# A sequence-mixing layer and a gated feed-forward on one core: another order for the opening

## The chip, the cores and the metric

The kernel runs on one core of a Trainium2 chip. The metric is the device time of one execution in microseconds; of several runs the median is given. A core has five engines with an instruction queue each, which work side by side and wait for each other through semaphores: TensorE (PE: matrix multiplications into PSUM), VectorE (DVE) and ScalarE (ACT) for elementwise work, GpSimd (POOL), and SyncE (SP), which here only issues DMA transfers. The output's transfers are issued from ScalarE's queue (L625).

## The reference, cut to what matters

A linear recurrence with a complex decay per channel, then a feed-forward whose hidden value is the product of two projections:

```python
mag = np.sqrt(a_re * a_re + a_im * a_im)
scale = np.minimum(mag, 0.999) / (mag + 1e-06)
a_re_n, a_im_n = (a_re * scale, a_im * scale)
...
for t in range(S):
    ar, ai = (a_re_n[:, :, t, :, None], a_im_n[:, :, t, :, None])
    new_re = ar * S_re - ai * S_im
    new_im = ar * S_im + ai * S_re
    kv = np.einsum('bhd,bhe->bhde', k[:, :, t], v[:, :, t])
    S_re, S_im = (new_re + kv, new_im)
    y[:, :, t] = np.einsum('bhd,bhde->bhe', q[:, :, t], S_re)
...
a = x @ w_a
b = x @ w_b
return (a * b @ w_out).astype(np.float32)
```

There are 4 sequences of 768 steps with 8 heads of 48 channels (3072 tokens of 384 values), a hidden width of 1536, and everything is float32.

## The kernel before, in words

The work is cut into 12 units (NU): two sequences by a chunk of 128 steps each. A unit goes through three parts.

*The elementwise part*, `prep(u)`, is VectorE's, with some ScalarE. `scale(u)` (L166) makes the factor that limits |a| from logarithms and exponentials: seven ScalarE instructions and five VectorE ones (L178, L185, L188, L190, L192), on a scratch tile `tmp`; for unit 0 in two halves. Then z = a * scale (L210), the running products of z over 16 steps (L223 to L234, one multiplication L226 and one addition L232 for each step; for unit 0 each in two halves), products over the blocks of 16 (L253, L259), their combination (L274, L279), an inverse square (L282 to L305), and q and k multiplied by the running products and their inverse (L294, L309). From unit 2 on, a unit's scale is made inside the part of the unit before it: in `prep(u)`, `scale(u + 1)` is drawn on by the loop over the 16 steps (L214, L234), with unit u's `a_t` as scratch. For units 0 and 1 this isn't so: unit 0's scale is issued by itself, and unit 1's stands at the head of `prep(1)` (L202, L203), with unit 0's `a_t` (`a_first`) as scratch. A unit's last act is to load `a_t` two units ahead (L317).

*The stacking and the attention*. `stack(u)` (L323) moves the products from 128 partitions, where heads cross partition borders, to one head per slice of `stk`, by ten DMA transfers from SBUF to SBUF, all issued by SyncE. `attn(u)` (L350) then yields after each of 18 pieces: scores (L364, masked on VectorE at L367), transposes (L375), outputs (L404), the rounding rest of the outputs (L412, L415), and the state for the next chunk (L423, L430).

*The feed-forward*, `gemm1` and `gemm2` for each of 12 blocks f of the hidden width (NF): 18 matmuls (L467) make a and b, ScalarE and VectorE make the product h and split it into a rounded value and a rest (L475 to L478), and six more matmuls (L485) add it to the output. Each operand is given to TensorE as two float32r parts, a rounded value and a rest, so the weights have to be split as well.

That splitting, `split_weights`, is a generator with one yield for each block f. A block has three parts (of w_a, w_b and w_out). For each, VectorE rebuilds the words with three instructions (L133, L135, L137; here called a conversion), ScalarE rounds (L141), TensorE subtracts (L146, L147), and ScalarE rounds the rest (L148). The words come by `load_weights(f)` (L121), three DMA transfers of 384 KB for a block.

The instructions are issued in the text's order to a tile framework, which allocates buffers, sets the semaphores and lays out each engine's queue; `tc.high_priority` moves a block of instructions ahead in that. The text's order around the change is this. Loads (L584 to L592): a of unit 0, weights of block 0, q and k of unit 0, block 1, v of unit 0, block 2, a of unit 1, then blocks 3 to 11. Then `scale(0)`, `prep(0)`, `stack(0)`, the load of q and k of unit 1, and the conversions of six blocks (CONV_FIRST). Then the pieces of `attn(0)`, with a part of `prep(1)` after each: `drain(gen, ns)` (L594) draws on a generator until the costs that it yields, in nominal ns, add up to ns; that is P1_A = 800 here. In the first turn of the main loop (w = 0) each block f is preceded by the next block's conversion and P1_F = 3000 of `prep(1)`; at f = P1_AT = 4 the rest of `prep(1)`, `stack(1)`, the load of q and k of unit 2 are issued and `prep(2)` is set up. `slot()` issues pieces of `attn(1)` from then on, spread over the blocks up to f = 11, where `prep(2)` and `stack(2)` are issued as a whole (L661 to L668). In later turns `prep` is drawn on by 2400 a block.

Of the kernel before, what the change touches and what calls it, by code (L numbers as in the profile page):

```python
# [22 lines left out]
NU = NBP * NCH  # L23
# [11 lines left out]
EPS = 1e-6  # L35
A2_MAX = 2.0 ** 60
ST = 8
P1_A = 800
P1_F = 3000
TOK = 2 * C  # L40
RUN = 2 * TOK + 2
NF = DF // 128
# [5 lines left out]
NCHK = NU * G + NU + 1  # L48
WPART = ((0, DM), (DM, DM), (2 * DM, DM))
CONV_FIRST = 6  # L50
P1_AT = 4
MOE_FIRST = 4000
ATTN_FIRST = 2000
ATTN_AT = (5, 6, 6, 6, 6)
# [12 lines left out]
def tile_kernel(ctx: ExitStack, tc: tile.TileContext, a_d, qk_d, v_d, w_d, qn_d, kn_d, vn_d, an_d, out_d):  # L67
    nc = tc.nc
    vec, act, pe, sync = nc.vector, nc.scalar, nc.tensor, nc.sync
# [35 lines left out]
    stk = const.tile([128, H, RUN], F32, name="stk")  # L105
    nc.gpsimd.memset(stk[KS:128], 0.0)
    qk = const.tile([128, NJ, 2, RUN], F32, name="qk")
# [13 lines left out]
    def load_weights(f):  # L121
        for m, (c0, n) in enumerate(WPART):
            raws[f, m] = wpool.tile([128, n, 2], U32, name=f"w{m}{f}")
            sync.dma_start(out=raws[f, m].rearrange("p c s -> p (c s)"),
                           in_=w_d[f, :, c0:c0 + n].bitcast(U32))
# [28 lines left out]
    def load_a(u):  # L154
        t = apool.tile([128, 2, W], F32, name="a_t")
        for hs in halves if u == 0 else (slice(0, W),):
            sync.dma_start(out=t[:, :, hs], in_=a_d[u, :, :, hs])
        return t

    a_tiles = {}  # L160
# [5 lines left out]
    def scale(u, a_t, tmp):  # L166

        sc = zpool.tile([128, W], F32, name="sc")
        for n, hs in enumerate(halves if u == 0 else (slice(0, W),)):
            n = n and NU
            t = tmp[:, 0:2, hs]
            m, x, s0 = t[:, 0], t[:, 1], sc[:, hs]
            act.activation(out=t, in_=a_t[:, :, hs], func=AF.Square, accum_out=sums[:, u + n:u + n + 1])
            vec.scalar_tensor_tensor(out=m, in0=m, scalar=-EPS * EPS, in1=x, op0=ALU.add, op1=ALU.add)  # L178
            act.activation(out=s0, in_=m, func=AF.Ln, bias=b_sq)
            act.activation(out=s0, in_=s0, func=AF.Exp, scale=0.5)  # L180
            act.activation(out=s0, in_=s0, func=AF.Ln, bias=b_eps)
            act.activation(out=s0, in_=s0, func=AF.Exp, scale=-1.0)
            act.activation(out=x, in_=s0, func=AF.Square)
            yield 900
            vec.tensor_tensor(out=m, in0=m, in1=x, op=ALU.mult)  # L185
            act.activation(out=x, in_=s0, func=AF.Identity, scale=-EPS, bias=b_one)
            yield 900
            vec.scalar_tensor_tensor(out=m, in0=m, scalar=-0.5, in1=x, op0=ALU.mult, op1=ALU.add)  # L188
            yield 900
            vec.scalar_tensor_tensor(out=s0, in0=m, scalar=0.5, in1=s0, op0=ALU.add, op1=ALU.mult)  # L190
            yield 900
            vec.scalar_tensor_tensor(out=s0, in0=s0, scalar=0.999, in1=x, op0=ALU.mult, op1=ALU.min)  # L192
            yield 900
        sc_tiles[u] = sc
# [4 lines left out]
    def prep(u):  # L199
        c = u % NCH  # L200
        a_t = a_tiles.pop(u)
        if u == 1:  # L202
            yield from scale(u, a_t, a_first)  # L203
            a_tiles[u + 1] = load_a(u + 1)
        sc = sc_tiles.pop(u)
        z = zpool.tile([128, 3, W], F32, name="z") if u else z_first
        zz = z[:]
# [3 lines left out]
                              in1=sc.rearrange("p (b i e) -> p b i e", e=2, i=SUB // 2), op=ALU.mult)  # L211
        act.activation(out=z[:, 0], in_=z[:, 2], func=AF.Copy, scale=-1.0)  # L212
        yield 1700
        sg = scale(u + 1, a_tiles[u + 1], a_t) if 0 < u < NU - 1 else iter(())  # L214


        zb = z.rearrange("p s (j b e) -> p s j b e", j=SUB // 2, e=2)
# [5 lines left out]
        for i in range(1, SUB):  # L223
            pr = small.tile([128, 2, 2, NB], F32, name="pr", bufs=1)
            for o, n in parts:
                vec.tensor_tensor(  # L226
                    out=pr[:, :, :, o:o + n],
# [23 lines left out]
        for sb in range(NSB):  # L251
            pb = small.tile([128, 2, 2, G], F32, name="pb")
            vec.tensor_tensor(  # L253
                out=pb,
# [16 lines left out]
        for k in range(2):  # L271
            pz = a_t
            for s in range(2):
                vec.tensor_tensor(  # L274
                    out=pz[:, s].rearrange("p (j b e) -> p j b e", j=SUB // 2, e=2), in0=zb[:, 1 + s],
# [38 lines left out]
        for k in range(2):  # L314
            times_p(k, 0 if u else 1, 2)
            yield 1670
        if 0 < u < NU - 2:  # L317
            a_tiles[u + 2] = load_a(u + 2)

    def load_qk(u):  # L320
        sync.dma_start(out=qk[:, :, 1, 0:2 * TOK], in_=qk_d[u])

    def stack(u):  # L323
        n = RUN if rescaled(u % NCH) else 2 * TOK
        for h in range(H):
            r0 = h * D
            while r0 < (h + 1) * D:
                j, p = divmod(r0, 128)
                m = min((h + 1) * D - r0, 128 - p)
                d0 = 2 * (r0 - h * D)  # L330
                sync.dma_start(out=stk[d0:d0 + 2 * m, h, 0:n], in_=qk[p:p + m, j, :, 0:n])
                r0 += m


# [249 lines left out]
    a_first = a_tiles[0] = load_a(0)  # L584
    load_weights(0)
    load_qk(0)
    load_weights(1)
    load_v(0)
    load_weights(2)
    a_tiles[1] = load_a(1)  # L590
    for f in range(3, NF):
        load_weights(f)  # L592

    def drain(gen, ns=None):  # L594
        if gen is None:
            return
        left = ns
        for cost in gen:
            if left is not None:
                left -= cost or 0  # L600
                if left <= 0:
                    return

    ws = split_weights()
    drain(scale(0, a_tiles[0], z_first))
    drain(prep(0))
    stack(0)
    load_qk(1)
    p1 = prep(1)
    for _ in range(CONV_FIRST):  # L610
        next(ws)
    x_cur = new_x()
    for _ in attn(0, *x_cur):
        drain(p1, P1_A)
    pend = []

    def second():
# [10 lines left out]
    for w in range(NU):  # L628
# [18 lines left out]
        for f in range(NF):  # L647
            if w == 0:
                next(ws, None)
                drain(p1, P1_F)  # L650
                if f == P1_AT:
                    drain(p1)
# [18 lines left out]
        x_cur = x_nxt  # L671
# [69 lines left out]
```

## Time and profile before

| what | value |
| --- | --- |
| runs | 701.16, 704.75, 705.05 us; median 704.75 |
| the profiled execution, its own time | 703.08 us |
| its span, first to last instruction | 701.3 us |
| mean granted TensorE clock | 0.981 |
| busy: PE, DVE, ACT, POOL | 654.5, 553.0, 319.0, 5.6 us |
| DMA: moved, mean rate | 63.95 MB, 91 GB/s |
| first matmul of scores, unit 0 (L364) | 64.20 us |
| first multiplication of the feed-forward, unit 0 (L467) | 80.86 us |
| first h of unit 1 (L476) | 153.09 us |

All times within the profile count from the span's start. A page gives the busy share of each engine in 40 slices, as tenths; the chain that ended last, followed back from the last instruction to what released it each time; and groups of instructions by source line. Views of the trace give the instructions of a stretch in order of time (start, duration, engine, line, operation, output and inputs, and in brackets the idle time before it and what ended it), sums over stretches, and who waited for whom. An instruction's duration reaches beyond the start of the next one where the two overlap in the engine's pipeline: what an instruction holds the engine for is read from start to start. PEld is TensorE's loading of the stationary operand. "SPq" is SyncE's queue, and the time given for a DMA there is that of its issue, not of the transfer.

### The profile page before, as it was taken

How to read it: one execution, taken by the hardware profiler on the slowest of the kernel's cores; microseconds unless marked ns; L12 is line 12 of the kernel's file. 1: busy time of each engine (PE TensorE's matmuls, PEld its weight loads, DVE VectorE, ACT ScalarE, POOL GpSimd, SP SyncE). 2: the span in 40 equal slices, each digit the busy share in tenths (PEclk: the TensorE clock that was granted, in tenths of full speed). 3: DMA queues.
4: the chain of work that ended last, by engine and by line, in shares of the span. 5: the costliest groups of instructions: out<-in, count | busy, mean ns of one | idle time of the engine just before them, and what ended most of it. 6: DMA issues, size and time to landing. Idle time of an engine off the chain costs nothing.

```text
span 701.3 us, 14492 instructions
## 1 busy us (share of the span) xinstructions
PE 654.5 (93%) x5862; PEld 608.7 (87%) x5862; DVE 553.0 (79%) x1387; ACT 319.0 (45%) x642; POOL 5.6 (1%) x11
## 2 busy tenths in 40 slices
PE   3657899999999999999999999999999999999997
PEld 1224788899898999999999998999999999999996
DVE  6999899898988989989799898999989963232221
ACT  6347666634635446255453554635543332232221
POOL 3000000000000000000000000000000000000000
PEclk9985999999999999999999999999999999999999
DMA  8963300511404206034051250511510510400000
GB/s 317 402 254 91 121 0 2 181 55 46 136 31 141 80 16 197 23 100 122 29 145 59 89 145 2 166 68 47 131 59 2 134 55 7 115 23 2 22 2 28
DMA packets 30233, 63.95 MB, mean 91 GB/s; under 512 B 3664, under 2 KB 7248, under 8 KB 30160
## 3 DMA queue, kind: packets, MB, share of 16 engines
q1 hardware_dynamic: 26704, 58.23, 26.4%
q10 hardware_dynamic: 3456, 4.72, 1.9%
q8 instruction: 48, 0.79, 0.5%
q14 instruction: 25, 0.20, 0.1%
HBM read 39.32 MB, written 4.72 MB: 63 GB/s over the span
## 4 chain that ended last, share of the span: by engine, by line
DVE 55%; PE 31%; ACT 6%; DMA 5%; issue 2%; SPq 0%; DVEq 0%; ACTq 0%
PE ab L467 13%; PE o L485 8%; DVE pr L226 6%; DVE qk L294 5%; DVE a_t L274 5%; DVE z L232 4%; DVE h_t L476 4%; DVE hl L478 4%; PE xp L404 3%; DMA w<-in_dram 3%; PE pm L364 3%; DVE z L279 3%; DVE pb L253 2%; DVE am L367 2%; DVE b_t L259 2%
## 5 line engine op out<-in xcount | busy, mean ns | idle before, releaser
L467 PE MATMUL ab<-xh,w 128*128 128x256 f32 x1728 | 332.5, 282 | 0.0
L467 PEld LDWEIGHTS ab<-xh,w 128*128 128x128 f32 x1728 | 275.6, 189 | 1.9 <-issue 1.0
L467 PE MATMUL ab<-xl,w 128*128 128x256 f32 x864 | 242.2, 280 | 0.0
L467 PEld LDWEIGHTS ab<-xl,w 128*128 128x128 f32 x864 | 162.6, 188 | 0.0
L485 PE MATMUL o<-w,hh 128*128 128x384 f32 x576 | 151.8, 344 | 0.0
L476 DVE TENSOR_TENSOR h_t<-ab,h_t 128x256 f32<-128x256 f32 x144 | 60.3, 419 | 71.3 <-ACT h_t L475 71.3
L475 ACT COPY h_t<-ab 128x256 f32<-128x256 f32 x144 | 53.0, 368 | 133.4 <-PE ab L467 132.3
L477 ACT CAST hh<-h_t 128x256 fp32r<-128x256 f32 x144 | 58.1, 404 | 107.9 <-DVE h_t L476 107.5
L485 PEld LDWEIGHTS o<-w,hh 128*128 128x128 f32 x576 | 96.5, 188 | 3.5 <-issue 3.4
L485 PE MATMUL o<-w,hl 128*128 128x384 f32 x288 | 97.8, 340 | 0.0
L478 DVE TENSOR_TENSOR hl<-h_t,hh 128x256 fp32r<-128x256 f32 x144 | 60.4, 419 | 18.0 <-ACT hh L477 17.8
L226 DVE TENSOR_TENSOR pr<-z 128x192 f32<-128x192 f32 (+1 forms) x195 | 65.2, 341 | 6.0 <-ACT z L212 1.2
L364 PE MATMUL pm<-stk 128*128 128x128 f32 x384 | 55.7, 283 | 4.9 <-DMA stk<-qk 4.3
L364 PEld LDWEIGHTS pm<-stk 128*128 128x128 f32 x384 | 50.2, 195 | 9.0 <-issue 6.4
L146 PE MATMUL ab<-o_sb,ident 128*128 128x384 f32 x42 | 30.6, 830 | 27.3 <-DVE o_sb L137 27.3
L485 PEld LDWEIGHTS o<-w,hl 128*128 128x128 f32 x288 | 54.1, 188 | 0.6 <-issue 0.4
L232 DVE TENSOR_TENSOR z<-pr 128x96 f32<-128x96 f32 (+1 forms) x195 | 47.2, 248 | 3.7
L404 PE MATMUL xp<-am,v_t 128*32 128x128 f32 x768 | 42.2, 277 | 3.8 <-DVE am L367 3.6
L274 DVE TENSOR_TENSOR a_t<-z,b_t 128x768 f32<-128x768 f32 x48 | 45.3, 950 | 0.0
L146 PEld LDWEIGHTS ab<-o_sb,ident 128*128 128x128 f32 x42 | 10.7, 296 | 37.3 <-DVE o_sb L137 27.3
L294 DVE TENSOR_TENSOR qk<-qk,z 128x1536 f32<-128x1536 f32 (+1 forms) x26 | 42.3, 1627 | 0.2
L367 DVE TENSOR_TENSOR am<-pm,mask 128x512 f32<-128x512 f32 x48 | 32.8, 684 | 6.8 <-PE pm L364 6.7
(100 smaller groups left out, 756.5 us busy)
## 6 DMA issues: line engine op xcount, KB each, us to landing
w<-in_dram SPq DMA_DIRECT2D x36, 384.0 KB, 7.9
qk<-in_dram SPq DMA_DIRECT2D x12, 768.0 KB, 4.8
stk<-qk SPq DMA_DIRECT2D x48, 192.0 KB, 3.3
a_t<-in_dram SPq DMA_DIRECT2D x11, 768.0 KB, 4.4
v_t<-in_dram SPq DMA_DIRECT2D x24, 256.0 KB, 2.7
stk<-qk SPq DMA_DIRECT2D x24, 192.8 KB, 3.3
out_dram<-o_sb ACTq DMA_DIRECT2D x24, 192.0 KB, 2.0
stk<-qk SPq DMA_DIRECT2D x16, 128.0 KB, 3.1
```

The source lines that it names most:

```text
L226: vec.tensor_tensor(out=pr[:, :, :, o:o + n], in0=view(zz, W + at_(i) + 2 * o, [[W, 2], [-W, 2], [2, n]]), in1=tok(slice(1, 3), i - 1, o, ...
L232: vec.tensor_tensor(out=tok(slice(1, 3), i, o, n), in0=pr[:, :, 0, o:o + n], in1=pr[:, :, 1, o:o + n], op=ALU.add)
L274: vec.tensor_tensor(out=pz[:, s].rearrange("p (j b e) -> p j b e", j=SUB // 2, e=2), in0=zb[:, 1 + s], in1=view(bb, (1 + k - s) * NB, [[0, ...
L294: vec.tensor_tensor(out=qk4[:, :, k, x0:x1], in0=qk4[:, :, 1, x0:x1], in1=z[:, k].rearrange("p (j t) -> p j t", j=NJ).unsqueeze(2).broadca ...
L364: pe.matmul(out=sp[:, h4], lhsT=stk[:, h, ks], rhs=stk[:, h, qs], start=True, stop=True)
L404: pe.matmul(out=xp[qd * 32:(qd + 1) * 32, ti], lhsT=l, rhs=rr, start=st, stop=sp_, tile_position=(0, qd * 32), skip_group_check=True)
L467: pe.matmul(out=ab[:, m * TOK:(m + 1) * TOK], lhsT=r(w_ab(f, part, m * NJ + i)), rhs=r(xt[:, i, :]), start=n == 0, stop=n == 8)
L475: act.copy(out=h_t, in_=ab[:, 0:TOK])
L476: vec.tensor_tensor(out=h_t, in0=ab[:, TOK:2 * TOK], in1=h_t, op=ALU.mult)
L477: act.copy(out=r(hh), in_=h_t)
L478: vec.tensor_tensor(out=r(hl), in0=h_t, in1=hh, op=ALU.subtract)
L485: pe.matmul(out=os_[tt][:, 0:DM], lhsT=r(ht[:, ts]), rhs=r(w_t[f, 2][:, part, :]), start=(f == 0 and n == 0), stop=(f == NF - 1 and n == 2))
```

## The change

Six things, all of the opening:

- `scale(1)` is no longer issued at the head of `prep(1)`. Like those of later units, it is drawn on within the step loop of the unit before, `prep(0)`, with unit 0's `a_t` as scratch. The load of unit 2's a moves with it, to the end of `prep(0)`.
- The load of unit 1's a stands ahead of the weights of block 1.
- The weights of blocks 3 to 5 are loaded behind `stack(0)`, those of blocks 6 to 11 behind the load of q and k of unit 1.
- Before `attn(0)` the conversions of three blocks are issued rather than six; those of blocks 3, 4 and 5 follow its 4th, 10th and 16th piece.
- `prep(1)` is not drawn on during `attn(0)` any more; in the first turn it gets P1_F = 2000 a block rather than 3000, and its rest and `stack(1)` come at f = 6 rather than 4.
- Of the transfers of `stack(0)` those of odd heads (five of ten) are issued by ScalarE.

```diff
--- before.py
+++ after.py
@@ -35,8 +35,7 @@
 EPS = 1e-6
 A2_MAX = 2.0 ** 60
 ST = 8
-P1_A = 800
-P1_F = 3000
+P1_F = 2000
 TOK = 2 * C
 RUN = 2 * TOK + 2
 NF = DF // 128
@@ -48,7 +47,7 @@
 NCHK = NU * G + NU + 1
 WPART = ((0, DM), (DM, DM), (2 * DM, DM))
 CONV_FIRST = 6
-P1_AT = 4
+P1_AT = 6
 MOE_FIRST = 4000
 ATTN_FIRST = 2000
 ATTN_AT = (5, 6, 6, 6, 6)
@@ -199,9 +198,6 @@
     def prep(u):
         c = u % NCH
         a_t = a_tiles.pop(u)
-        if u == 1:
-            yield from scale(u, a_t, a_first)
-            a_tiles[u + 1] = load_a(u + 1)
         sc = sc_tiles.pop(u)
         z = zpool.tile([128, 3, W], F32, name="z") if u else z_first
         zz = z[:]
@@ -211,7 +207,7 @@
                               in1=sc.rearrange("p (b i e) -> p b i e", e=2, i=SUB // 2), op=ALU.mult)
         act.activation(out=z[:, 0], in_=z[:, 2], func=AF.Copy, scale=-1.0)
         yield 1700
-        sg = scale(u + 1, a_tiles[u + 1], a_t) if 0 < u < NU - 1 else iter(())
+        sg = scale(u + 1, a_tiles[u + 1], a_t) if u < NU - 1 else iter(())
 
 
         zb = z.rearrange("p s (j b e) -> p s j b e", j=SUB // 2, e=2)
@@ -314,7 +310,7 @@
         for k in range(2):
             times_p(k, 0 if u else 1, 2)
             yield 1670
-        if 0 < u < NU - 2:
+        if u < NU - 2:
             a_tiles[u + 2] = load_a(u + 2)
 
     def load_qk(u):
@@ -328,7 +324,7 @@
                 j, p = divmod(r0, 128)
                 m = min((h + 1) * D - r0, 128 - p)
                 d0 = 2 * (r0 - h * D)
-                sync.dma_start(out=stk[d0:d0 + 2 * m, h, 0:n], in_=qk[p:p + m, j, :, 0:n])
+                (act if u == 0 and h % 2 else sync).dma_start(out=stk[d0:d0 + 2 * m, h, 0:n], in_=qk[p:p + m, j, :, 0:n])
                 r0 += m
 
 
@@ -584,12 +580,10 @@
     a_first = a_tiles[0] = load_a(0)
     load_weights(0)
     load_qk(0)
+    a_tiles[1] = load_a(1)
     load_weights(1)
     load_v(0)
     load_weights(2)
-    a_tiles[1] = load_a(1)
-    for f in range(3, NF):
-        load_weights(f)
 
     def drain(gen, ns=None):
         if gen is None:
@@ -605,13 +599,18 @@
     drain(scale(0, a_tiles[0], z_first))
     drain(prep(0))
     stack(0)
+    for f in range(3, CONV_FIRST):
+        load_weights(f)
     load_qk(1)
+    for f in range(CONV_FIRST, NF):
+        load_weights(f)
     p1 = prep(1)
-    for _ in range(CONV_FIRST):
+    for _ in range(3):
         next(ws)
     x_cur = new_x()
-    for _ in attn(0, *x_cur):
-        drain(p1, P1_A)
+    for n, _ in enumerate(attn(0, *x_cur)):
+        if n % 6 == 3:
+            next(ws)
     pend = []
 
     def second():
```

## The prediction

> **What bounds the kernel now.** I read the page first: the busy shares in 40 slices and the chain that ended last.
>
> ```profile
> span 701.3 us, 14492 instructions
> ...
> PE   3657899999999999999999999999999999999997
> ...
> DVE  6999899898988989989799898999989963232221
> ...
> PEclk9985999999999999999999999999999999999999
> ...
> DVE 55%; PE 31%; ACT 6%; DMA 5%; issue 2%; SPq 0%; DVEq 0%; ACTq 0%
> ```
>
> A slice is 17.5 us. TensorE is full from the sixth slice (88 us) on, and not before; VectorE is nearly full from the second slice to the 32nd, and it is VectorE that the chain follows for 55% of the span. So there are two bounds, and the next view, sums over stretches that I cut at three events, says which one holds where: the first stacking transfer of unit 0 (60.66), that of unit 1 (126.86), and the end of unit 1's attention, about 150.3.
>
> ```profile
> 8.00:60.60 52.60, 32.92 (x57) 14.79 (x57) 51.91 (x163) 27.17 (x54) 0.00 (x0) 0.86 0.75 292
> 60.60:126.90 66.30, 61.84 (x440) 53.18 (x441) 62.25 (x152) 41.84 (x86) 0.00 (x0) 0.93 0.22 68
> 126.90:150.30 23.40, 22.08 (x261) 19.55 (x260) 20.95 (x53) 13.88 (x24) 0.00 (x0) 1.00 0.44 131
> 150.30:657.00 506.70, 498.62 (x4823) 482.71 (x4822) 406.19 (x988) 220.71 (x444) 0.00 (x0) 1.00 0.26 76
> ```
>
> The columns are PE, PEld, DVE, ACT, POOL, then clock and DMA. From 150.3 on TensorE is busy for 498.62 of 506.70 and VectorE for 406.19: that part is TensorE's, and the change leaves it alone. What the change can move is the moment at which unit 1's multiplications begin. Up to unit 1's stacking VectorE is busy for 51.91 + 62.25 = 114.2 of the 118.9 us after 8 us; it idles 0.69 and 4.05. That is the number I build on: **unit 1's stacking starts when VectorE has worked through its list**, and the chain in order of time confirms the hand-over:
>
> ```profile
> 125.17 1.67 DVE qk L294
> 126.86 3.42 DMA stk<-qk
> 130.32 0.49 PE pm L364 x2
> ```
>
> What is on that list? The weight conversions, by three instructions each (here the third, L137; a window's row has its busy time and count):
>
> ```profile
> 0.00:60.60 60.60, 10.37 (x19) 0.88 0.74 282
> 60.60:126.90 66.30, 8.72 (x16) 0.93 0.22 68
> 126.90:150.30 23.40, 0.55 (x1) 1.00 0.44 131
> ```
>
> 35 of 36 conversions are done before unit 1's stacking, 19 of them before unit 0's, though the text issues them after it. So text order isn't engine order. The timeline of VectorE shows how they get there:
>
> ```profile
> 20.52 0.33 DVE L232 TENSOR_TENSOR z<-pr 128x48 f32<-128x48 f32 x2
> 20.76 0.55 DVE L137 SCALAR_TENSOR_TENSOR o_sb<-w,o_sb 128x384 uint32<-128x384 uint32 x1
> 21.23 0.42 DVE L226 TENSOR_TENSOR pr<-z 128x96 f32<-128x96 f32 x2
> ```
>
> One conversion instruction sits after each step of unit 0's recurrence: 0.47 us from start to start for L137. Whoever laid the queues out filled each place where the next step wasn't ready with anything that was.
>
> **The change part by part.**
>
> *Weight loads 3 to 11 issued behind unit 0's stacking.* If the SP queue kept the text's order, these 27 loads would start only after the stacking, and their conversions would have to stay behind it. The queue's timeline speaks against that:
>
> ```profile
> 13.94 26.16 SPq L124 DMA_DIRECT2D w<-in_dram  x27
> 60.66 6.75 SPq L331 DMA_DIRECT2D stk<-qk  x10
> ...
> 145.46 5.08 SPq L340 DMA_DIRECT2D v_t<-in_dram  x2
> 170.63 0.33 SPq L157 DMA_DIRECT2D a_t<-in_dram  x1
> 174.58 6.71 SPq L331 DMA_DIRECT2D stk<-qk  x10
> ```
>
> Unit 2's v (145.46) stands in the text behind unit 4's a (170.63) and unit 2's stacking (174.58), since L633 of the second turn follows L665 of the first. It was issued 25 and 29 us ahead of them, because they weren't ready. Loads 3 to 11 need nothing at all, so I expect them where they are now, from 14 to 40 us, the first of them about 2 us later, since unit 1's a_t stands ahead of block 1's weights and is as large as two of these loads (26.16 for 27 is 0.97 each). Cost nothing, gain nothing, and the conversions of blocks 3 to 5 fill the same places as now.
>
> *Unit 1's scale within unit 0's part.* Five VectorE instructions and seven on ScalarE, now around and behind 60 us, move to between 20 and 42 us:
>
> ```profile
> 60.55 0.95 DVE L178 SCALAR_TENSOR_TENSOR a_t<-a_t 128x768 f32<-128x768 f32 x1
> ...
> 70.40 0.96 DVE L188 SCALAR_TENSOR_TENSOR a_t<-a_t 128x768 f32<-128x768 f32 x1 [0.54 <-ACT a_t L186]
> 71.39 0.96 DVE L190 SCALAR_TENSOR_TENSOR sc<-a_t,sc 128x768 f32<-128x768 f32 x1
> 72.27 0.68 DVE L367 TENSOR_TENSOR am<-pm,mask 128x512 f32<-128x512 f32 x1
> ```
>
> Each holds the engine 0.88 (from 71.39 to 72.27). Where one takes the place of a conversion instruction (0.47), unit 0's stacking gets 5 x 0.41 = 2.1 us later; where it is squeezed in besides, 5 x 0.88 = 4.4. I take the lower end, since 19 conversions of three instructions found places before the stacking and five places are all it needs, so about 63, with two conversions fewer done by then. To unit 1's stacking this is worth nothing: the list has the same instructions in another order. What it saves is the wait of 0.54 above, where the scale ran alone. ScalarE, 27.17 busy of 52.60 before 60.6, has the room.
>
> *Unit 2's a_t* is now asked for ahead of the stacking: one issue of 0.33 us in the same queue, as the row at 170.63 has it. It is free once L309 has read unit 0's, 2 us before the stacking is due, so the stacking waits 0 to 0.3; I take 0.
>
> *Stacking by two engines.* Ten issues take SP 6.75 us; five each take 3.4, so the last rows arrive 3.3 us sooner. On ScalarE five issues cost up to 5 x 0.68 = 3.4 of its own time, during which its casts wait. The waits of VectorE that this may shorten:
>
> ```profile
> DVE am L367 <- PE pm L364: 0.7, 1, 0.7
> ...
> DVE o_sb L133 <- PE pm L364: 0.6, 1, 0.6
> ```
>
> The two, 1.3 together, are the wait for the first scores. With the list otherwise unchanged I take 1.0 of them as gained: the first unit's multiplications then begin some 2 us sooner, 2.1 later and about 4 earlier (3.3 and the large scale instructions no longer in front of the mask at 72.27).
>
> [...]
>
> *P1_F 2000 and P1_AT 6*: unit 1's part stands later in the text, behind all conversions. 35 of 36 are ahead of the end already; the last third of a conversion (0.47) may join them: +0.5.
>
> *Behind unit 1's stacking.* The 23.4 us to 150.3 hold the last block of multiplications besides the attention. Unit 0's attention, with none, took from 60.66 to
>
> ```profile
> 80.86 0.36 PE L467 MATMUL ab<-xh,w 128*128 128x256 f32 x1
> ```
>
> which is 20.2. If the multiplications are all done by then, up to 3.2 falls away; TensorE starts 2 us sooner but shares VectorE's list, so I take 1.0.
>
> **The sum**: -0.5 (scale's wait) -1.0 (first scores) +0.5 (order) -1.0 (after the stacking) = -2.0. The profiled execution took 703.08 (span 701.3 and 1.8 around it); the runs shown are 701.16, 704.75 and 705.05. I set the sum against the mean of these four, 703.5, which is 0.4 above the profiled one and 1.2 below the runs' median: **701.5 us**. Its own range: at best all 4.05 of idle and 3.2 behind go (696.2), at worst ScalarE's 3.4 shows up as waits (705).
>
> **The rivals.**
>
> *The conversions do stay behind* (the change does what its name says; my SP reading is wrong). Then by the stacking only 9 are done instead of 19. One costs 1.2 (0.27 + 0.47 + 0.47, start to start), so ten are 12; less the scale's 4.4, the stacking is at 53, the multiplications begin near 70, and TensorE runs ahead of VectorE all the way to unit 1's stacking. This still can't start before VectorE has done its 114.2 us of list: the gain is the idle time, 4.05, and the 3.2 behind, 7.3 in all: **696.2**. For it: the loads stand behind the stacking in the text. Against it: v at 145.46.
>
> *Unit 1's chain without filling* (slower). With the conversions all ahead in priority and 13 of its 27 us (nominal, the drained costs) issued in one go at block 6, unit 1's part runs last and alone. Then nothing fills its waits for ScalarE. In later units, where no conversions are left, they look like this:
>
> ```profile
> DVE a_t L288 <- ACT a_t L282: 10.3, 10, 1.6
> ...
> DVE a_t L303 <- ACT a_t L290: 4.9, 8, 1.9
> ```
>
> 1.0 and 0.6 for each of them. And the recurrence, 15 steps of an L226 and an L232, holds the engine longer when nothing stands between. Unit 1's at present, first unfilled, then filled:
>
> ```profile
> 78.91 0.36 DVE L226 TENSOR_TENSOR pr<-z 128x192 f32<-128x192 f32 x1
> 79.30 0.26 DVE L232 TENSOR_TENSOR z<-pr 128x96 f32<-128x96 f32 x1
> ...
> 96.93 0.34 DVE L226 TENSOR_TENSOR pr<-z 128x192 f32<-128x192 f32 x1
> 97.20 0.55 DVE L137 SCALAR_TENSOR_TENSOR o_sb<-w,o_sb 128x384 uint32<-128x384 uint32 x1
> ```
>
> 0.39 against 0.27 from start to start; with the same 0.12 for each of the 30 that is 3.6. Together +5.2: **708.7**. It decides from the point where the conversions end before L288 of unit 1. Now they fill those places:
>
> ```profile
> 115.70 0.96 DVE L288 TENSOR_TENSOR a_t<-a_t 128x768 f32<-128x768 f32 x1
> ...
> 116.91 0.56 DVE L135 SCALAR_TENSOR_TENSOR o_sb<-w,o_sb 128x384 uint32<-128x384 uint32 x1
> ```
>
> For it: the blocks' order in the text. Against it: VectorE's list isn't shorter, so something is left to fill with.
>
> **How the numbers follow.** My forecast has 0.50, the first rival 0.25, the slower one 0.15, and 0.10 is for a new order in later units, either way. A measurement of this kernel tells about 1% from no change, 7 us: below 697.7 or above 711.8 against the runs' median. Faster by that: 0.16 from the first rival, 0.07 from the forecast's good end, 0.05 from the rest, 0.28. Slower: 0.06 from the slower rival, 0.06 from the rest and from ScalarE's casts, 0.12. Same: 0.60. The range goes from 694.5 (first rival and a little) to 709.5 (slower rival and a little).
>
> **What would show it.** Right: in the SP queue the 27 loads still run from about 14 to 42 us ahead of the stacking; 16 to 18 L137 stand before it; its first issue is at 62 to 65, five issues on each of two queues in 3.5 us; unit 1's stacking at 123 to 128 with VectorE idle 2 to 4 us in between; from there on everything shifted alike. Wrong: a first stacking near 53 (the loads were held back), unit 1's stacking before 121 (VectorE's list isn't the bound, or conversions were put behind it), or beyond 130 with waits for ScalarE at L288 and L303.

## The result, and the profile after

The changed kernel takes 713.76 us (median of four runs, 713.58 to 714.36), the kernel before 703.81 (four runs, 701.16 to 705.05): the ratio is 1.0137, with an interval of 1.0117 to 1.0157. The forecast was 701.5 in a range of 694.5 to 709.5, so the change is slower, beyond the range. The profiled execution took 713.67 with a span of 711.9.

The page of the changed kernel first, in the lines that were shown of the kernel before.

```profile
span 711.9 us, 14484 instructions
...
PE   2356999899999999999999999999999999999996
...
DVE  6998899878998999989889898999989963223221
...
PEclk9565999979999999999999999999999999999999
...
DVE 49%; PE 36%; ACT 6%; DMA 5%; issue 2%; SPq 1%; DVEq 0%; ACTq 0%
```

A slice is 17.8 us. Behind the first 88 us two things are new: PE has an 8 in the eighth slice (125 to 142 us), and the row PEclk has a 7 in the ninth (142 to 160). Both were 9 before. (PEclk is lower in the second and third slices as well, 5 and 6 against 9 and 8. The time doesn't follow that part: of the changed kernel's four executions the one with the highest mean clock, 0.976, took longest, 714.36 us.) TensorE, which before was full from 88 us on, now runs dry once more, at the place of unit 1's attention.

The same sums over stretches, cut at the changed kernel's own events (first stacking transfer of unit 0, of unit 1, first multiplication of unit 1; columns as before: PE, PEld, DVE, ACT, POOL, clock, DMA):

```profile
8.00:64.00 56.00, 28.04 (x51) 12.65 (x51) 54.47 (x162) 30.14 (x57) 0.00 (x0) 0.66 0.72 280
64.00:134.80 70.80, 69.08 (x481) 58.95 (x482) 62.55 (x156) 39.88 (x87) 0.00 (x0) 0.93 0.21 60
134.80:160.40 25.60, 21.28 (x221) 17.08 (x220) 20.15 (x52) 12.42 (x20) 0.00 (x0) 0.80 0.42 120
160.40:667.00 506.60, 498.99 (x4825) 482.79 (x4824) 405.64 (x986) 220.49 (x444) 0.00 (x0) 1.00 0.26 76
```

The last row is the same as before to 0.1 us (506.70 then). All the loss lies in the opening, and the cuts divide it: unit 0's stacking 3.4 us later (60.66 to 64.07), the stretch between the stackings 4.6 longer (66.2 to 70.8), the stretch from unit 1's stacking to its first h 2.6 longer (26.23 to 28.86): 10.6 in all, which is what the span grew by. VectorE's work up to unit 1's stacking is 54.47 + 62.55 = 117.0 (114.2 before), its idle time 1.53 + 8.25 (0.69 + 4.05). Where VectorE idles between the stackings (line, what it waited for, us in all, times, longest):

```profile
DVE am L363 <- PE pm L360: 2.2, 3, 1.5
DVE o_sb L132 <- ACT w L140: 1.9, 1, 1.9
```

These two, and 0.6 more for a mask, lie at unit 0's attention (68 to 79 us); 2.2 more lie behind 120 us and come next.

The conversions, by their third instruction (busy, count), and the SP queue:

```profile
0.00:64.00 64.00, 9.39 (x18) 0.70 0.72 272
64.00:134.80 70.80, 10.23 (x19) 0.93 0.21 60
134.80:160.00 25.20, 0.00 (x0) 0.80 0.43 122
```

```profile
9.89 30.44 SPq L123 DMA_DIRECT2D w<-in_dram  x30
61.65 0.33 SPq L156 DMA_DIRECT2D a_t<-in_dram  x1
64.07 4.00 SPq L327 DMA_DIRECT2D stk<-qk  x5
...
134.85 7.94 SPq L327 DMA_DIRECT2D stk<-qk  x10
```

(One of the 19 straddles the cut; there are 36 in all.) The loads did stay where they were, 10 to 40 us, and 18 conversions stand before unit 0's stacking, one fewer than before. What differs is the other end, here on VectorE's timeline:

```profile
110.77 0.55 DVE L136 SCALAR_TENSOR_TENSOR o_sb<-w,o_sb 128x384 uint32<-128x384 uint32 x1
...
124.36 0.96 DVE L284 TENSOR_TENSOR a_t<-a_t 128x768 f32<-128x768 f32 x1 [0.78 <-ACT a_t L278]
...
126.61 0.43 DVE L474 TENSOR_TENSOR hl<-h_t,hh 128x256 fp32r<-128x256 f32 x1 [0.96 <-ACT hh L473]
127.46 0.96 DVE L299 TENSOR_TENSOR a_t<-a_t 128x768 f32<-128x768 f32 x1 [0.42 <-ACT a_t L286]
...
134.74 0.41 DVE L472 TENSOR_TENSOR h_t<-ab,h_t 128x256 f32<-128x256 f32 x1
```

The last conversion and unit 0's last h in the kernel before:

```profile
127.42 0.55 DVE L137 SCALAR_TENSOR_TENSOR o_sb<-w,o_sb 128x384 uint32<-128x384 uint32 x1
...
132.67 0.41 DVE L476 TENSOR_TENSOR h_t<-ab,h_t 128x256 f32<-128x256 f32 x1
```

110.77 is the last of all conversions; before the change the last came at 127.4. Behind it unit 1's chain has nothing to fill its waits for ScalarE (L284 and L299 are L288 and L303 of the kernel before). And 134.74 is the last h of unit 0: it comes with the start of unit 1's stacking (134.85), where before it came 5.8 us after it (132.7 against 126.86). So unit 0's multiplications are over when unit 1's attention begins. TensorE in three stretches of 10 us, and what it waited for between 120 and 160 us, each followed by a row of the kernel before (the middle stretch; the same 40 us):

```profile
130.00:140.00 10.00, 8.18 (x49) 6.96 (x47) 9.72 (x16) 4.36 (x8) 0.00 (x0) 1.00 0.57 165
140.00:150.00 10.00, 7.50 (x52) 5.78 (x56) 6.80 (x19) 5.42 (x8) 0.00 (x0) 0.60 0.63 185
150.00:160.00 10.00, 10.00 (x156) 8.74 (x149) 8.02 (x21) 3.08 (x6) 0.00 (x0) 0.88 0.11 36
```

```profile
140.00:150.00 10.00, 9.49 (x161) 8.49 (x149) 9.47 (x25) 3.94 (x8) 0.00 (x0) 1.00 0.23 75
```

```profile
PE pm L360 <- DMA stk<-qk: 3.7, 4, 1.8
PE pm L360 <- ACT kt L375: 0.6, 1, 0.6
```

```profile
PE pm L364 <- DMA stk<-qk: 0.7, 1, 0.7
```

It waits for the stacked rows with nothing else to do, and its granted clock falls. The 0.60 and 0.88 are averages over these cuts: from 142.1 to 152.2 the clock is 0.50, and from 140 to 142 and from 152.4 to 160 it is 1.00. As an estimate from these rows: idle time from 130 to 150 us is 1.82 + 2.50 = 4.3 (none from 120 to 130; 1.3 in these 30 us before), and busy time at the lower clock loses 7.50 x 0.40 + 10.00 x 0.12 = 4.2; together 7.2 more than before. With the 2.3 by which unit 0's first multiplication is late (83.13 against 80.86) that is 9.5 of the 10.6. Ahead of the stretch at 0.50 lie waits of 1.07, 1.78 and 0.53 us between 137.2 and 142.1. The loss of clock that counts here is at unit 1's attention.

### The profile page after: what moved, and what is told of

Read it like the earlier page. It is cut to its first block, busy times and chain, and to the rows that moved or that the text cites. A ratio compares the mean times of both kernels' runs of the same rounds, so it can differ in the third digit from the quotient of the medians.

```text
span 711.9 us, 14484 instructions
## 1 busy us (share of the span) xinstructions
PE 656.7 (92%) x5862; PEld 610.2 (86%) x5862; DVE 555.0 (78%) x1387; ACT 318.7 (45%) x642; POOL 5.6 (1%) x11
## 4 chain that ended last, share of the span: by engine, by line
DVE 49%; PE 36%; ACT 6%; DMA 5%; issue 2%; SPq 1%; DVEq 0%; ACTq 0%
PE ab L463 15%; PE o L481 7%; DVE qk L290 5%; DVE pr L222 5%; DVE a_t L270 5%; PE pm L360 4%; PE xp L400 4%; DVE h_t L472 4%; DVE z L228 4%; DVE hl L474 4%; DMA stk<-qk 2%; DVE z L275 2%; DVE pb L249 2%; DMA w<-in_dram 2%; PE pm L419 2%
## 5 line engine op out<-in xcount | busy, mean ns | idle before, releaser
L472 DVE TENSOR_TENSOR h_t<-ab,h_t 128x256 f32<-128x256 f32 x144 | 60.3, 419 | 71.0 <-ACT h_t L471 70.9
L360 PE MATMUL pm<-stk 128*128 128x128 f32 x384 | 58.8, 291 | 8.9 <-DMA stk<-qk 8.3
L145 PE MATMUL ab<-o_sb,ident 128*128 128x384 f32 x42 | 29.1, 796 | 35.6 <-DVE o_sb L136 35.6
L290 DVE TENSOR_TENSOR qk<-qk,z 128x1536 f32<-128x1536 f32 (+1 forms) x26 | 42.3, 1627 | 0.2
```

The source lines that it names most:

```text
L290: vec.tensor_tensor(out=qk4[:, :, k, x0:x1], in0=qk4[:, :, 1, x0:x1], in1=z[:, k].rearrange("p (j t) -> p j t", j=NJ).unsqueeze(2).broadca ...
L360: pe.matmul(out=sp[:, h4], lhsT=stk[:, h, ks], rhs=stk[:, h, qs], start=True, stop=True)
L472: vec.tensor_tensor(out=h_t, in0=ab[:, TOK:2 * TOK], in1=h_t, op=ALU.mult)
```

## The experiments

The table has every kernel that ran. "Chain" is the first addition (L232) of unit 1's recurrence on VectorE, "S0" and "S1" the first stacking transfers of units 0 and 1, "last h" is unit 0's, all us from the span's start, of the profiled execution; "PE, clock" is TensorE's busy time and granted clock in the 40 us from 120 to 160. Times are medians, ratios are to the kernel before, run beside it.

| kernel | S0 | chain | S1 | last h | PE, clock | us | ratio and interval |
|---|---|---|---|---|---|---|---|
| before | 60.7 | 78.6 | 126.9 | 132.7 | 38.7, 1.00 | 703.81 | |
| after | 64.1 | 77.5 | 134.9 | 134.7 | 35.7, 0.87 | 713.76 | 1.0137 (1.0117 to 1.0157) |
| e1 after, one engine | 63.6 | 72.1 | 131.9 | 133.0 | 37.4, 1.00 | 708.69 | 1.0086 (1.0063 to 1.0108) |
| e2 before, two engines | 60.3 | 82.0 | 133.0 | 127.9 | 33.0, 0.87 | 711.3 | 1.0120 (1.0092 to 1.0148) |
| e3 after, old plan | 64.2 | 73.5 | 127.5 | 135.7 | 39.4, 1.00 | 707.54 | 1.0064 (1.0043 to 1.0084) |
| e4 after, loads back | 63.9 | 76.6 | 134.0 | 133.9 | 36.0, 0.91 | 713.58 | 1.0156 (1.0137 to 1.0176) |
| e5 before, scale alone | 64.1 | 67.2 | 121.1 | 148.8 | 39.7, 1.00 | 706.78 | 1.0059 (1.0037 to 1.0082) |
| e6 before, new plan | 60.9 | 79.9 | 134.4 | 129.3 | 32.3, 0.87 | 711.77 | 1.0135 (1.0106 to 1.0165) |
| e7 after, blocks held | 57.6 | 73.5 | 137.0 | 134.9 | 34.8, 0.91 | 717.43 | 1.0216 (1.0191 to 1.0240) |
| e8 before, P1_AT 2 | 59.5 | 77.6 | 126.1 | 131.9 | 38.7, 1.00 | 703.19 | 1.0008 (0.9988 to 1.0027) |
| e9 after, blocks at 7, 8, 9 | 64.5 | 77.8 | 127.4 | 159.0 | 33.1, 0.87 | 715.11 | 1.0172 (1.0148 to 1.0196) |
| e10 as e6, blocks at 7, 8, 9 | 60.5 | 79.6 | 125.9 | 159.3 | 30.4, 0.79 | 713.53 | 1.0145 (1.0121 to 1.0169) |
| e11 before, blocks at 5, 6, 7 | 60.7 | 77.3 | 124.8 | 158.7 | 32.6, 0.79 | 712.23 | 1.0137 (1.0115 to 1.0159) |
| e12 as e1, blocks at 7, 8, 9 | 63.9 | 71.5 | 122.3 | 158.4 | 35.8, 0.83 | 711.83 | 1.0129 (1.0107 to 1.0150) |
| e13 after, blocks all at 7 | 64.8 | 77.5 | 128.4 | 136.6 | 40.0, 1.00 | 705.61 | 1.0039 (1.0023 to 1.0055) |
| e14 as e6, blocks all at 7 | 60.2 | 79.2 | 127.2 | 133.8 | 38.6, 1.00 | 704.66 | 1.0024 (1.0004 to 1.0044) |
| e15 before, blocks all at 5 | 60.0 | 76.5 | 124.9 | 130.7 | 38.7, 1.00 | 703.02 | 1.0006 (0.9988 to 1.0024) |
| e16 as e1, blocks all at 7 | 64.6 | 73.0 | 124.4 | 148.0 | 39.7, 1.00 | 707.65 | 1.0058 (1.0039 to 1.0077) |
| e17 as e2, blocks all at 5 | 60.8 | 82.8 | 133.7 | 128.6 | 33.1, 0.87 | 710.69 | 1.0109 (1.0083 to 1.0134) |
| e18 as e13, scale back | 59.5 | 90.8 | 138.2 | 129.4 | 29.4, 0.74 | 716.58 | 1.0189 (1.0164 to 1.0214) |

The column of the clock divides them: each kernel in which TensorE keeps 1.00 takes 703.0 to 708.7 us, each in which it doesn't 710.7 to 717.4. What goes with it is the place of unit 0's last h. In the nine kernels that keep the clock it comes 1.1 to 27.8 us behind S1; in the others it comes ahead of S1, by 0.1 to 8.8 us, or more than 31 us behind it (e9 to e12).

**The parts one by one.** Unit 0's stacking issued by SyncE alone, in the changed kernel:

```diff
-(act if u == 0 and h % 2 else sync).dma_start(out=stk[...], in_=qk[...])
+sync.dma_start(out=stk[...], in_=qk[...])
```

> The changed kernel (713.8 us) with one part undone: all ten transfers of unit 0's stacking are issued by SyncE again. My theory: the loss of 10 us has two causes, the five issues on ScalarE (5.9 us in its queue, with weight casts held behind them and VectorE waiting for a cast for 1.9 us) and the plan that puts unit 1's elementwise part behind the conversions. By it this run gains 2 to 4 us: 710 to 712. Rival, the plan is the only cause: no gain, 713 to 714.5. Rival, two issuing engines do help and only something else hurts: 715 to 717.

The opposite edit in the kernel before:

```diff
-sync.dma_start(out=stk[...], in_=qk[...])
+(act if u == 0 and h % 2 else sync).dma_start(out=stk[...], in_=qk[...])
```

> The kernel before (703.8 us) with one part of the change alone: the odd heads' five transfers of unit 0's stacking issued by ScalarE. My theory (ScalarE's casts are held up and VectorE waits for them): 2 to 4 us slower, 706 to 708. Rival (the rows arrive 3.3 us sooner, as predicted): 701 to 703.

The old plan of unit 1's part in the changed kernel (P1_A, P1_F, P1_AT and the two loops around unit 0's attention as before):

```diff
-P1_F = 2000
+P1_A = 800
+P1_F = 3000
-P1_AT = 6
+P1_AT = 4
...
-    for n, _ in enumerate(attn(0, *x_cur)):
-        if n % 6 == 3:
-            next(ws)
+    for _ in attn(0, *x_cur):
+        drain(p1, P1_A)
```

> The changed kernel with the earlier plan for unit 1's part and the conversions: 800 ns of it after each piece of unit 0's attention, 3000 for each block, the rest and the stacking at block 4, six blocks of conversions ahead of the attention. Unit 1's scale within unit 0's part and the two issuing engines stay. My theory (the plan costs about 6 of the 10 us): 706 to 709, and unit 1's stacking begins before 131 us instead of 134.9. Rival (unit 0's stacking 3.4 us later, through the scale in unit 0's part, is what is passed on): 712 to 714, with unit 1's stacking still near 135.

Loads 3 to 11 back in their old place of the text:

```diff
     load_weights(2)
+    for f in range(3, NF):
+        load_weights(f)
```

> The changed kernel with the loads of the weights of blocks 3 to 11 back where the kernel before has them, ahead of everything of unit 0. My theory (the place of the loads in the text doesn't matter, since they are issued as soon as the queue is free): 713 to 714.5, the same. Rival (the later place of the loads costs something): 708 to 712.

Only scale(1) and the load of its a_t changed (e1's, e3's and e4's edits together in the changed kernel):

> The kernel before with one part of the change alone: unit 1's scale drawn on within unit 0's part (with the loads of unit 1's and unit 2's a where the change has them). Stacking by SyncE, the earlier plan for unit 1's part, weight loads as before. My theory (this part only puts the same instructions in another order, unit 0's stacking 3 us later and unit 1's not): 702 to 705. Rival (the later stacking of unit 0 is passed on): 706 to 708.

The new plan alone in the kernel before (e3's edit the other way):

```diff
-P1_A = 800
-P1_F = 3000
+P1_F = 2000
-P1_AT = 4
+P1_AT = 6
...
```

> The kernel before with one part of the change alone: the plan (three blocks of conversions before unit 0's attention, one after its 4th, 10th and 16th piece, unit 1's part only in the first turn with 2000 a block, its rest and the stacking at block 6). My theory (with unit 1's part behind all conversions its chain runs unfilled and the multiplications are over before unit 1's stacking): 707 to 710, unit 1's stacking at 131 to 134. Rival (the plan hurts only together with the new place of the scale): 702 to 704.

Measured: the loads are worth nothing (713.58 against 713.76), so that reading of the queue holds. Undoing the second engine gives 5 us back, undoing the plan 6; yet the second engine alone costs 8.4, the plan alone 8.5, the scale alone 3.5, each against the kernel before run beside it. So the costs don't add: either of the first two alone brings most of the loss. The rows of the two single parts for 120 to 160 us, e2 and then e6, show the same picture as the changed kernel's:

```profile
120.00:160.00 40.00, 33.01 (x322) 29.54 (x322) 34.80 (x89) 18.05 (x30) 0.00 (x0) 0.87 0.34 103
```

```profile
120.00:160.00 40.00, 32.32 (x317) 28.99 (x316) 34.90 (x87) 18.11 (x29) 0.00 (x0) 0.87 0.34 102
```

Unit 0's last h is 5 us ahead of S1 in both. e5 tells a second thing: S1 comes 5.8 us earlier than before the change, and the kernel is still slower. So an early stacking by itself gained nothing here, with TensorE busy for 39.7 of the 40 us.

**Conversions held behind on purpose.** The first rival made real: blocks 3 to 11 wait on VectorE until unit 0's last product (L290) has been issued.

```diff
+                with tc.issue_after(held[0].ins) if f > 2 else ExitStack():
                     vec.tensor_scalar(out=tu, in0=raw[:, :, 1], ...)
...
-            vec.tensor_tensor(
+            held[u] = vec.tensor_tensor(
                 out=qk4[:, :, k, x0:x1], ...
```

> The changed kernel, with the conversions of blocks 3 to 11 queued on VectorE behind unit 0's last product, as the change's name says: nothing else differs. The prediction's first rival: unit 0's stacking near 53, unit 1's not before VectorE has worked through the same list, 122 to 127 if nothing is lost; time 696 to 706. My theory now (a chain without filling holds VectorE longer, and the conversions missing from the first chain come ahead of the second): unit 0's stacking at 50 to 54, unit 1's at 128 to 134, 706 to 713.

And unit 1's chain written earlier in the kernel before (earlier than the old plan had it):

```diff
-P1_AT = 4
+P1_AT = 2
```

> The kernel before with one number changed: the rest of unit 1's part and its stacking are issued at block 2 rather than 4, ahead of the conversions of blocks 9 to 11. My theory (what counts is the order on VectorE before unit 1's stacking; conversions behind it can be done beside unit 1's attention): unit 1's stacking 4 to 9 us sooner, 697 to 702. Rival (the conversions come along as filling anyway): 702 to 705.

Measured: e8 is no different. In e7 the conversions do stay behind (third instructions before unit 0's stacking and between the stackings):

```profile
0.00:57.60 57.60, 4.98 (x9) 0.67 0.80 299
57.60:137.00 79.40, 14.78 (x27) 0.94 0.19 55
```

Unit 0's stacking comes 6.4 us sooner than in the changed kernel, but the 27 that were moved now lie between the stackings, S1 is at 137.0, and by its median the kernel is the slowest of all, with e18 close to it.

**The last three blocks behind unit 1's chain.** My theory after these: the plan lets all 36 conversions run ahead of unit 1's chain. The test writes blocks 9 to 11 later in unit 0's loop, everything else as changed.

```diff
             if w == 0:
-                next(ws, None)
+                if f < 3 or f > P1_AT:
+                    next(ws, None)
                 drain(p1, P1_F)
```

> The changed kernel with one edit: the conversions of blocks 9, 10 and 11 are written behind unit 1's chain (at f = 7, 8, 9 of unit 0's loop) instead of at f = 3, 4, 5. Everything else, the two engines and scale(1) included, as in the changed kernel. Theory (the conversions that run ahead of unit 1's chain are what unit 1 lacks): 80 or so of the 108 conversion instructions stand ahead of the end of unit 1's recurrence, as before the change, not 108; VectorE's idle time between the two stackings falls from 8.25 us to about 4 to 5; unit 1's stacking starts by 129 and the stretch from unit 0's stacking to unit 2's first h takes 143 to 145 us (150.6 in the changed kernel, 143.3 before). Time 706 to 708.5, so what is left against before is the 3.4 us by which unit 0's stacking is late. Rival (the two engines' block on ScalarE and the wait for the scores set it, where the conversions stand is immaterial): 712 to 714.

> The kernel before with the changed kernel's plan (711.77 so), and blocks 9 to 11 written behind unit 1's chain. Neither scale(1) nor the second engine is moved, so unit 0's stacking starts at about 61. Theory (conversions ahead of the chain alone are the cost of the plan): 703 to 705, stretch from unit 0's stacking to unit 2's first h 143 to 145 us (150.9 without the edit). Rival (what the plan costs is that unit 1's chain is drawn out to f = 6, at 2000 a step): 709 to 712.

> The kernel before, unit 1's plan untouched, blocks 9 to 11 written behind unit 1's chain (f = 5, 6, 7) instead of at f = 3, 4, 5. Theory by its size: unit 1's chain there idles 4.05 us between the stackings and TensorE, not VectorE, sets the stretch of 143.3 us behind unit 0's stacking, so little is to be had: 701.5 to 704. If VectorE's idle time were the bound there as well: about 699 to 701. If TensorE runs out of converted blocks: 705 to 708.

> The changed kernel with all stacking on SyncE (708.69 so) and blocks 9 to 11 written behind unit 1's chain. Theory (TensorE's own work sets 143.4 us from unit 0's stacking to unit 2's first h, and unit 0's stacking starts at 63.6 to 64.1 because of scale(1)): 705.5 to 707.5, 1 to 3 us under the same kernel without the edit. Rival (the cost of the second engine is separate and additive, 5 us): 702 or less.

S1 came to 122 to 127, as foreseen, but the time fell in none of them. It rose clearly in e11 (against the kernel before) and e12 (against e1); in e9 and e10 the intervals overlap those of the changed kernel and of e6. All four came out above every time that had been named for them, so theory and rivals missed. The timeline of VectorE in e9 and TensorE's longest wait there say why.

```profile
143.92 0.57 DVE L136 SCALAR_TENSOR_TENSOR o_sb<-w,o_sb 128x384 uint32<-128x384 uint32 x1
...
145.75 0.55 DVE L136 SCALAR_TENSOR_TENSOR o_sb<-w,o_sb 128x384 uint32<-128x384 uint32 x1
```

```profile
PE pm L360 <- DMA stk<-qk: 5.9, 3, 5.5
```

The last block had fallen into unit 1's attention (its conversions end at 144.6 to 146.1 in the four), so in e9 unit 0's last multiplications began at 150.0 us, and TensorE was dry again at the same place, from the other side. So the theory was too narrow: what has to be right isn't how early S1 is, but that multiplications of unit 0 are left, and possible, while unit 1's rows are stacked. The next four write the three blocks in one place, right behind the chain and ahead of unit 1's attention.

```diff
-                next(ws, None)
+                for _ in range(3 if f == P1_AT + 1 else f < 3):
+                    next(ws, None)
```

> The changed kernel with the conversions of blocks 9 to 11 all written at f = 7, right behind unit 1's chain and ahead of unit 1's attention. Theory (TensorE runs dry beside unit 1's attention when its last multiplications of unit 0 are done by the start of unit 1's stacking, and also when their blocks are converted too late): unit 1's stacking by 129.5 (134.85 in the changed kernel), block 11 converted by 130, unit 0's last h behind the start of the stacking and before 142, PE busy for over 28 of the 30 us from 120 to 150 (25.7 in the changed kernel, 28.7 before); time 706 to 709. Rival (the chain drawn out to f = 6 and the two engines cost by themselves, wherever the conversions stand): 711 to 715.

> The kernel before with the changed kernel's plan (711.77) and blocks 9 to 11 together right behind unit 1's chain. Theory: 702 to 706. Rival (the drawn out chain by itself): 709 to 712.

> The kernel before with blocks 9 to 11 together at f = 5, right behind unit 1's chain. That is near what its order gives anyway (9 of 36 conversions behind the recurrence): 701.5 to 705. If 706 or more, the time hangs on single conversions more finely than the theory has it.

> The changed kernel with all stacking on SyncE (708.69) and blocks 9 to 11 together right behind unit 1's chain. Theory: 705 to 708, no longer better than the same with two engines by more than 2 us; rival (the second engine costs 5 us by itself): 5 us under e13, so 701 to 704 if e13 is 706 to 709.

Measured: this one edit takes the changed kernel from 1.0137 to 1.0039 (1.0023 to 1.0055), and the plan alone from 1.0135 to 1.0024. The views of e13: TensorE from 120 to 160 us, the conversions by stretch, and VectorE where unit 1's chain ends.

```profile
120.00:160.00 40.00, 40.00 (x396) 36.62 (x395) 37.84 (x96) 21.35 (x44) 0.00 (x0) 1.00 0.34 104
```

```profile
0.00:64.80 64.80, 9.47 (x18) 0.71 0.72 268
64.80:128.30 63.50, 9.14 (x17) 0.95 0.23 66
128.30:160.00 31.70, 1.11 (x2) 1.00 0.36 106
```

```profile
119.88 0.55 DVE L136 SCALAR_TENSOR_TENSOR o_sb<-w,o_sb 128x384 uint32<-128x384 uint32 x1
...
120.91 0.95 DVE L299 TENSOR_TENSOR a_t<-a_t 128x768 f32<-128x768 f32 x1
...
122.98 0.55 DVE L136 SCALAR_TENSOR_TENSOR o_sb<-w,o_sb 128x384 uint32<-128x384 uint32 x1
```

TensorE is busy for all 40.00 us at a granted clock of 1.00; L299 no longer waits, since a conversion stands before it; two conversions are left for after S1. The place of three blocks alone takes back about 7 of the changed kernel's 10 us, and most of the plan's 8.5. That settles the cause of most of the loss: the blocks' early place, through a TensorE that has nothing to multiply while unit 1's rows are stacked. It isn't a rule that early conversions always cost this: in e1 all of them stand ahead of the end of unit 1's recurrence too (the last at 107.7), but S1 comes 1.1 us ahead of the last h, the clock stays at 1.00, and moving the blocks (e16) changes little, 1.0058 against 1.0086. e16 has a last h at 148 and is no better than e13, so the second engine is no separate cost of 5 us; e15, nearest to the kernel before, is the same as it.

**What the second engine does.** Two more: e2 with e15's edit, and e13 with scale(1) back at the head of unit 1's part:

```diff
         a_t = a_tiles.pop(u)
+        if u == 1:
+            yield from scale(u, a_t, a_first)
+            a_tiles[u + 1] = load_a(u + 1)
...
-        sg = scale(u + 1, a_tiles[u + 1], a_t) if u < NU - 1 else iter(())
+        sg = scale(u + 1, a_tiles[u + 1], a_t) if 0 < u < NU - 1 else iter(())
...
```

> The kernel before with the second engine for unit 0's stacking (711.3 so) and blocks 9 to 11 together at f = 5, right behind unit 1's chain. Theory (the second engine costs nothing by itself; what it did was to let the last conversions slip ahead of unit 1's chain, so that TensorE ran dry later): 701.5 to 705, PE busy over 38 of the 40 us from 120 to 160 at clock 1.00 (33.0 at 0.87 without the edit). Rival (the second engine's hold on ScalarE costs by itself): 708 to 712.

> The changed kernel with blocks 9 to 11 right behind unit 1's chain (705.6 so) and unit 1's scale back at the head of unit 1's part: both engines, the plan and the loads stay as changed. Theory (what is left against before is scale(1) in unit 0's part, by unit 0's stacking being 3 to 4 us later): 702 to 704.5, ratio to before within 0.2%. Rival (what is left is of the other edits): 705 to 706.5.

Both theories missed: e17 came out where its rival had it, e18 beyond either. In e17 the edit did not move the conversions (the last at 114.5, S1 at 133.7), nor in e18 (116.7), so they say nothing of the conversions; but both show what else holds unit 1's chain. ScalarE and VectorE of e18 behind unit 0's stacking:

```profile
59.65 5.58 ACTq L330 DMA_DIRECT2D stk<-qk  x5
65.33 1.34 ACT L140 CAST w<-o_sb 128x384 fp32r<-128x384 f32 x3 [5.27 <-DMA stk<-qk]
66.58 0.93 ACT L178 ACTIVATE sc<-a_t,biases 128x768 f32<-128x768 f32 x1
```

```profile
77.76 0.96 DVE L184 TENSOR_TENSOR a_t<-a_t 128x768 f32<-128x768 f32 x1 [2.05 <-ACT a_t L182]
80.73 0.96 DVE L187 SCALAR_TENSOR_TENSOR a_t<-a_t 128x768 f32<-128x768 f32 x1 [2.01 <-ACT a_t L185]
```

While ScalarE issues its five transfers (5.58 us) it computes nothing for 5.27 us. Where unit 1's scale stands behind the stacking, six of its seven ScalarE operations wait for that, and the chain starts late: 78.6 to 82.0 (e2), 76.5 to 82.8 (e17 against e15), 90.8 (e18). With scale(1) moved, the second engine delays the chain too (72.1 to 77.5, e1 and after; 73.0 to 77.5, e16 and e13), but the scale is done. So moving the scale costs 3.5 us alone, and saves 10 to 11 where the second engine and the new plan are in (e18 against e13).

## Why the prediction was wrong, point by point

*Loads 3 to 11: cost nothing.* Right: 30.44 us from 9.89, and e4 is the same. Only the delay of 2 us had no ground, as unit 1's a stood ahead of these loads before as well: they end at 40.3, and at 40.1 before.

*Scale(1) within unit 0's part: the lower end, 2.1, stacking at 63.* It took 3.4, to 64.07: nearer to the upper end, 4.4, less the one conversion that was displaced. "Worth nothing to unit 1's stacking" did not hold: alone (e5) it brings S1 5.8 us forward, to 121.1, with 33 conversions and eight h done by then (35 and ten before). The time rises all the same, 1.0059.

*Unit 2's a_t: 0.* Right; issued at 61.65, well ahead.

*Stacking by two engines: rows 3.3 us sooner, -1.0.* Failed. The DMA listings of the kernel before and after, for the 192 KB issues of this stacking (count, size, median us to landing):

```profile
stk<-qk SPq DMA_DIRECT2D x6, 192.0 KB, 3.2
```

```profile
stk<-qk SPq DMA_DIRECT2D x3, 192.0 KB, 5.1
stk<-qk ACTq DMA_DIRECT2D x3, 192.0 KB, 5.3
```

The issues were shared out, but landing grew by 2 us. The last row landed 9.0 us after the first issue, against 9.4 before (8.6 in e2), so of the 3.3 us only 0.4 to 0.8 came. The wait for the first scores, 1.3 us of which 1.0 was to be gained, grew instead: the two rows of VectorE's waits above and the 0.6 make 4.7, and with the second engine undone (e1) 1.1 of that is left. What made the landing longer no run isolates. ScalarE's side was under-sized as well, 3.4 against:

```profile
64.07 5.92 ACTq L327 DMA_DIRECT2D stk<-qk  x5
...
70.04 1.34 ACT L140 CAST w<-o_sb 128x384 fp32r<-128x384 f32 x3 [7.60 <-DMA stk<-qk]
70.59 0.36 DVE L132 TENSOR_SCALAR o_sb<-w 128x384 uint32<-128x384 uint32 x1 [1.93 <-ACT w L140]
```

*P1_F 2000 and P1_AT 6: +0.5.* This is the step that failed most: "35 of 36 are ahead of the end already". The count at S1 was the wrong count. Before, 27 of the third instructions stand ahead of the end of unit 1's recurrence, and nine are left to fill what follows (the last at 127.4); after, all 36 stand ahead of it (the last at 110.8). So the multiplications of unit 0 that depend on them are over when unit 1's rows are stacked, and TensorE runs dry. Put at +0.5 us, the plan alone costs 8.5 (e6, 1.0135), and with the blocks put back 1.0024 (e14). The count at the recurrence is no rule either: e2 and e14 both have 30 there, and take 711.30 and 704.66 us.

*Behind unit 1's stacking: -1.0, since no multiplications would be in the way.* Wrong in sign, +2.6. The multiplications that e13 has beside unit 1's attention don't slow it, and TensorE keeps its clock (1.00 from 120 to 160 us, 0.87 in the changed kernel): from S1 to unit 1's first h it takes 25.0 us, the changed kernel 28.9. With unit 0's last h later than in e13 it does take longer (27.9 in e16, 32.4 in e5). The same matmuls for the scores (mean ns of one), from 120 to 165 us, after and in e13:

```profile
L360 PE MATMUL pm<-stk 128*128 128x128 f32 x32 | 8.0, 368 | 4.3 <-DMA stk<-qk 3.7 <-ACT kt L375 0.6
```

```profile
L360 PE MATMUL pm<-stk 128*128 128x128 f32 x32 | 5.3, 285 | 0.0
```

*The leading idea: unit 1's stacking starts when VectorE has worked through its list, and the list is conserved.* Neither half carries the end. The list up to S1 grew by 2.9 us, because all twelve h and the last conversion were done in it, instead of ten h; and S1 alone doesn't set the time (e5, e9, e12).

*The rivals.* "Unit 1's chain without filling" came nearest: the sign, S1 beyond 130, and waits at L288 and L303 (1.2 us, 1.6 forecast). But its larger term, 3.6 for a recurrence with nothing between its steps, did not come, as the conversions ran within the recurrence (it ends at 111.9, they at 110.8). It lacked the waits at unit 0's attention and the dry TensorE behind S1. That its 708.7 lies nearest is thus luck in part. "The conversions do stay behind", forecast at 696.2, is the slowest arrangement when made (e7): 57.6 for S0 and not 53, and 717.4. "From there everything shifted alike" held: from unit 1's first h to unit 2's are 50.9 us in both kernels.

*What stays open.* The 0.39% (0.23 to 0.55) that e13 keeps against before: scale(1)'s place doesn't explain it simply, as e18 shows. Why e3, e5 and e16, with TensorE full up to 160 us, take 54.7 to 57.9 us from unit 1's first h to unit 2's (in e16 the clock is 0.92 and 0.91 in the 10 us on either side of 180, which is not enough for it). And by what the second engine alone lets the conversions end at 116 (e2): the late chain fits, but no run made the chain later without ScalarE (e5 made it 11 us earlier). No kernel here beats the one before; e8 and e15 equal it.

## What to carry to other kernels

Work that fills the waits of one stage should not be counted as done when it is early: count what will be left to fill the next stage, for each engine, and look there first at the one that bounds the rest of the span (here TensorE beside unit 1's attention). Too early and too late cost much the same: with the last conversions done by 111 us or only at 146, the changed kernel lost 10 and 12 us; with them done by 132 (e13), 3. Before a transfer is issued from a second engine, compare time to landing with time to issue, and see what that engine would have computed meanwhile.

## What the runs showed of the hardware

- In the changed kernel three waits of TensorE, of 1.07, 1.78 and 0.53 us between 137.2 and 142.1, were followed by a granted clock of 0.50 from 142.1 to 152.2. In e1, where TensorE was busy for 37.35 of the 40 us from 120 to 160, one wait of 1.73 us up to 135.3 and two of 0.30 and 0.57 at 139 and 142 left the clock at 1.00. In e18, with a wait of 9.3 us, it was 0.50 from 140 to 150.
- With ten transfers within SBUF issued from two engines, those of 192 KB took 4.2 to 5.3 us to landing (medians, e2 and after) instead of 3.2; all ten had landed 8.6 (e2) and 9.0 us (after) after the first issue, against 9.4 from one engine.
- Five issues on ScalarE's queue took 4.76 (e2) to 5.92 us (the changed kernel), where the five beside them on SyncE took 4.00 (the changed kernel) and 4.21 (e7); ScalarE computed nothing for 4.39 us beside them in e2, for 5.27 in e18.
